# The last phase of a gated spectral/GEGLU backward kernel: the first way-back piece after two gate jobs, three kinds of loads on ScalarE's queue, ten b tiles ahead

## The chip, the cores and the metric

The kernel runs on one core of one Trainium2 chip. The metric is the device time of one execution in microseconds. Before the change the median of three runs is 1390.53 us (1386.52 to 1390.64).

The engines named below are TensorE (PE; its weight loads are PEld), VectorE (DVE), ScalarE (ACT), GpSimd (POOL) and SyncE (SP). Each executes its own instructions in order. DMA transfers are issued by SyncE, ScalarE or GpSimd, as one more instruction in that engine's stream; SPq, ACTq and POOLq mark these in the profile.

## The reference

```python
def _A_ref(x, w_r, w_i):                      # spectral mixer
    X = rfft2(x.astype(float32)); X = X * (w_r + 1j * w_i)
    return irfft2(X, s=(S, D)).astype(bfloat16)
def _B_ref(x, w_gate, w_up, w_down):          # GEGLU
    return (gelu(x @ w_gate) * (x @ w_up)) @ w_down
x = A_x
g = sigmoid((x * gate_w).sum(-1, keepdims=True))
out = g * _A_ref(x, A_w_r, A_w_i) + (1 - g) * _B_ref(x, B_w_gate, B_w_up, B_w_down)
# returned: out, and its vector-Jacobian product with grad_out for
# x, w_r, w_i, w_gate, w_up, w_down, gate_w
```

x and grad_out are 2048 x 576, w_gate and w_up 576 x 4608, w_down 4608 x 576, the spectral weights 2048 x 289, all in bfloat16.

## The kernel before, in words

The 2048 rows are 16 row tiles t of 128 rows. The kernel has two phases.

The first phase (up to 919.7 us in the profile) goes through the 4608 hidden columns in 18 groups of 256. It computes the hidden activations and their gradients, stores them to DRAM scratch (`scr`, three kinds: A for the down product, dHg and dHu for the two gradients), accumulates the three weight gradients, and in between performs the forward transforms of x and grad_out, the products with the spectral weights, and the first half of the transforms back. Their half-way result lies in DRAM as V (`scr_p1` for the output, `scr_p2` for the gradient of x).

The second phase, in which the whole change lies, makes the output and the gradient of x. Its work is a list of jobs, one at a time on TensorE (L1123 to L1126):

- a b job (`b_job`, L1301) multiplies row tile t of A with the down weights `wd_all`, in three `pin` tiles of 12 chunks, two blocks each (one for each half of the 576 columns). A block is 12 matmuls (L1194). ScalarE copies the result into `bo`;
- a g job and a u job (`x_half`) accumulate the gradient of x for row tile t, first from dHg with `wgT_all`, then from dHu with `wuT`, into one PSUM pair that is held from the g job to the end of the u job. `x_end` then has VectorE add the spectral part and the gate part to it (`x_pre` L1366, `x_out` L1371) and store it.

The order before is g0, g1, b0 to b7, u0, u1, b8, and then g_t, u_t, b_(t+7) for t from 2, without b when they are used up. The last row tile's g and u are one job ("x").

The pin tiles are loaded by transposing DMA on SyncE's queue (L1120), six buffers, always six ahead of the block that TensorE has finished (`ensure`). The order of these loads is the order of the jobs. On the same queue, ahead of the jobs, stand three loads of `wd_all` (L1139) and the first loads of V; one transposing load of a quarter of a third of `wuT` (L1153, 9 in all) stands ahead of each of the jobs 1 to 9.

Between the blocks lie the pieces of the way back, four for each row tile i (`piece`, L1259): k = 0 and 1 are `z_piece` for the output and the gradient (six matmuls of the folded V, called F, with the table `RT`, L1244, and a copy Z by ScalarE, L1246); k = 2 and 3 are `d_piece` (six matmuls of Z with the table `It`, L1254, and two ScalarE activations into `yo`, kept in `spec[0]` or `spec[1]`, L1256). A piece also issues what comes later: k = 0 and 1 load V for row i + 2 (`load_p`, L1210, on SyncE's queue), k = 1 and 2 have VectorE fold V of row i + 1 into F (`fold`, L1221 to L1237), and k = 3 calls `posts`. The tables RT and It are built at the start of the phase from GpSimd iotas, VectorE arithmetic in float tiles (`f32t`) and ScalarE sines (L222, L203).

`tick` (L1283) decides when a piece comes. It is called after each block; its counter advances by one, except in g0 and g1, where no b job has begun and it stays. A piece is taken when the counter has reached a threshold, which starts at 0 and is then moved 3 or 4 ahead. So the first piece comes after the first block of g0, and a row takes 14 blocks.

`post(t)` (L1314) is done once b job t and the row's output piece are there. It loads x and grad_out of the row tile (L1319, L1321, SyncE's queue), and has VectorE make the output row, the gate's derivative (`dlog`, from grad_out, L1331) and the gradient of gate_w (from x, L1335). `x_end(t)` needs `dlog` of its row.

PSUM gives the phase eight tiles, four pairs, shared by b jobs, gate and up jobs and pieces (`acc_pair`).

Of the kernel before, what the change touches and what calls it, by code (L numbers as in the profile page):

```python
# [11 lines left out]
BF16 = mybir.dt.bfloat16  # L12
# [7 lines left out]
S, D, DF = 2048, 576, 289  # L20
P, T = 128, 16
# [22 lines left out]
def eo(c):  # L44

    return slice(c, 512, 4)
# [278 lines left out]
def kernel(  # L325
# [4 lines left out]
    nc = tc.nc  # L330
    LD = nc.sync
# [3 lines left out]
    kw = dict(reuse_waits="tile")  # L335
# [9 lines left out]
    x_v = A_x[0].rearrange("(p t) d -> p t d", t=T)  # L345
    do_v = grad_out[0].rearrange("(p t) d -> p t d", t=T)
# [523 lines left out]
    for c in range(6):  # L870
        w = gwr[0:1, eo(c)] if c < 4 else gwr[0:1, 512:D]
# [58 lines left out]
    def want(pr):  # L930

        n0 = FIRST[-1]
        if pr < len(FIRST):
            return FIRST[pr]

        def load(n):

            return n + 0.5 * min(max(n - mid_at, 0), n_mid)
        share = load(n0) + (load(n_slots) - load(n0)) * (pr + 1 - len(FIRST)) / (LASTP - len(FIRST))
        n = n0  # L940
        while n < n_slots and load(n + 1) <= share + 1e-9:
            n += 1
        return int(min(n, n_slots) + 1e-9)
# [21 lines left out]
    for g in range(NG):  # L965
# [3 lines left out]
        for m in range(NPR):  # L969
            pr = g * NPR + m  # L970
            n = want(pr) - done[0]
# [64 lines left out]
            else:  # L1036
# [29 lines left out]
                jobs = carry + hs  # L1066
# [53 lines left out]
        LD.dma_start_transpose(tl[:], scr[k][t // 4][t % 4][:, f0 * P:(f0 + FCB) * P])  # L1120
        return tl

    jobs = [("g", t) for t in range(2)] + [("b", t) for t in range(8)] + [("u", t) for t in range(2)] + [("b", 8)]  # L1123
    for t in range(2, T):
        jobs += [("g", t), ("u", t)] + ([("b", t + 7)] if t + 7 < T else [])
    jobs[-2:] = [("x", T - 1)]  # L1126
    seq = [(k, t, f0) for kind, t in jobs for k in ((1, 2) if kind == "x" else ("bgu".index(kind),)) for f0 in range(0, NFC, FCB)]
    loaded = {}
# [25 lines left out]

    o0v = out_0[0].rearrange("(p t) d -> p t d", t=T)
    o1v = out_1[0].rearrange("(p t) d -> p t d", t=T)
    with tc.tile_pool(name="p2f", bufs=4, **kw) as p2f, \
         tc.tile_pool(name="p2bo", bufs=8, **kw) as p2bo, \
         tc.tile_pool(name="p2b", bufs=6, **kw) as p2b, \
         tc.tile_pool(name="sp", bufs=1, **kw) as sp, \  # L1160
         tc.tile_pool(name="p2s", bufs=4, **kw) as p2s, \
         tc.tile_pool(name="p2res", bufs=1, **kw) as p2res, \
# [11 lines left out]
        def f32t(dt=F32):  # L1174
            return p2f.tile([P, D], dt, tag="f32t", name="f32t")

        def b16t():
            return p2b.tile([P, D], BF16, tag="b16t", name="b16t")
# [9 lines left out]
        def acc_pair():  # L1188
            return [pacc.tile([P, 512], F32, tag="acc", name="acc") for _ in range(2)]
# [14 lines left out]
        srcs_v = [q[:].rearrange("g (k t c) l -> (g k) t c l", k=4, c=2) for q in (scr_p1, scr_p2)]  # L1204
        vp, ft, zt = {}, {}, {}
        spec = [{}, {}]

        def load_p(i, w):
            vp[i, w] = sp.tile([P, 2, DF], BF16, tag="Vp", name="Vp", bufs=4)
            LD.dma_start(vp[i, w][:], srcs_v[w][:, i])  # L1210

        def fold(i, w):
            v = vp.pop((i, w))
# [33 lines left out]

        def d_piece(i, w):
            Z = zt.pop((i, w))
            yo = spec[w][i] = sp.tile([P, D], BF16, tag=("ya", "yd")[w], name="yo", bufs=(3, 6)[w])  # L1250
            yv = yo[:].rearrange("p (q r) -> p r q", r=6)
            for b, ps in enumerate(acc_pair()):
                for r in range(3):
                    nc.tensor.matmul(ps[:, r * 96:(r + 1) * 96], lhsT=Z[0:2 * LQ, 3 * b + r, :], rhs=It[0:2 * LQ, 3 * b + r, :],  # L1254
                                     start=True, stop=True)
                nc.scalar.activation(yv[:, 3 * b:3 * b + 3], ps[:, 0:288].rearrange("p (r q) -> p r q", r=3), ACT.Copy,  # L1256
                                     scale=(SD2, 1.0)[w])

        def piece(i, k):  # L1259

            def f():
                (z_piece, d_piece)[k // 2](i, k % 2)
                if k == 0 and i + 2 < T:
                    load_p(i + 2, 0)
                if k == 1:
                    if i + 2 < T:
                        load_p(i + 2, 1)
                    if i + 1 < T:
                        fold(i + 1, 0)
                if k == 2 and i + 1 < T:  # L1270
                    fold(i + 1, 1)
                if k == 3:
                    posts()
            return f
        pieces = [piece(i, k) for i in range(T) for k in range(4)]
        for i in range(2):
            for w in range(2):
                load_p(i, w)
        for w in range(2):
            fold(0, w)  # L1280
        ticks = [0, 0]

        def tick(on):  # L1283
            ticks[0] += on
            if pieces and ticks[0] >= ticks[1]:
                pieces.pop(0)()
                ticks[1] = ticks[0] + 3 + len(pieces) % 2

# [2 lines left out]
                pieces.pop(0)()  # L1291

        bos = {}
        posted = [0]

        def posts():
            while posted[0] in bos and posted[0] in spec[0]:
                post(posted[0])
                posted[0] += 1

        def b_job(t):  # L1301
            bps = acc_pair()
            bo = bos[t] = p2bo.tile([P, D], BF16, tag="bo", name="bo")
            for f0 in range(0, NFC, FCB):
                At = loaded.pop((0, t, f0))
                for h in range(2):
                    block(bps[h], h, At, lambda r: wd_all[:, f0 + r], f0 == 0, f0 + FCB == NFC)
                    tick(1)
                    if f0 + FCB == NFC:
                        nc.scalar.copy(bo[:, h * 288:(h + 1) * 288], bps[h][:, :288])  # L1310
                used[0] += 1
                ensure()

        def post(t):  # L1314

            bo = bos.pop(t)
            a_t = spec[0][t]
            x_t = b16t()
            LD.dma_start(x_t[:], x_v[:, t, :])  # L1319
            do_t = b16t()  # L1320
            LD.dma_start(do_t[:], do_v[:, t, :])  # L1321
            tmpo = f32t()
            V.tensor_scalar(tmpo[:], bo[:], omg32[:, t:t + 1], None, op0=ALU.mult)
            o0 = b16t()
            V.scalar_tensor_tensor(o0[:], a_t[:], g32[:, t:t + 1], tmpo[:], op0=ALU.mult, op1=ALU.add)
            ST.dma_start(o0v[:, t, :], o0[:])
            diff = f32t()
            V.tensor_tensor(diff[:], a_t[:], bo[:], op=ALU.subtract)
            junk = f32t()
            dg = p2s.tile([P, 1], F32, tag="dg", name="dg")  # L1330
            V.scalar_tensor_tensor(junk[:], diff[:], 1.0, do_t[:], op0=ALU.mult, op1=ALU.mult, accum_out=dg[:])  # L1331
            gg = p2s.tile([P, 1], F32, tag="gg", name="gg")
            V.tensor_tensor(gg[:], g32[:, t:t + 1], omg32[:, t:t + 1], op=ALU.mult)
            V.tensor_tensor(dlog[:, t:t + 1], dg[:], gg[:], op=ALU.mult)
            V.scalar_tensor_tensor(gacc[:], x_t[:], dlog[:, t:t + 1], gacc[:], op0=ALU.mult, op1=ALU.add)  # L1335
            if t == T - 1:
                V.tensor_copy(gsplit[:, 0], gacc[:])
                V.tensor_tensor(gsplit[:, 1], gacc[:], gsplit[:, 0], op=ALU.subtract)
# [12 lines left out]
        def x_half(t, k):  # L1351
            if k == 1:
                accs[t] = acc_pair()
            for f0 in range(0, NFC, FCB):
                src = loaded.pop((k, t, f0))
                for h in range(2):
                    block(accs[t][h], h, src, wT(k, f0), k == 1 and f0 == 0, k == 2 and f0 + FCB == NFC)
                    tick(len(bos) + posted[0] > 0)
                used[0] += 1
                ensure()  # L1360
# [81 lines left out]
```

## Time and profile before

| | us |
|---|---|
| median of three runs | 1390.53 |
| lowest, highest | 1386.52, 1390.64 |
| profiled execution | 1392.35 |
| its span, first to last instruction | 1390.6 |
| TensorE busy (weight loads) | 1366.5 (906.6) |
| VectorE, ScalarE, GpSimd busy | 842.9, 751.4, 260.5 |
| second phase, start to end | 919.7 to 1390.6 |
| mean granted TensorE clock | 0.993 |

The busy times are sums over the span; TensorE's overlapping weight loads are counted by themselves. The granted clock is the share of the full TensorE clock that the throttle allowed. A view of waits has one row for each pair of a waiting line and the one that released it: total time, number, longest. A timeline row has the start, the length, the engine, the line, the operation, what it writes and reads, how often, and in brackets the idle time of its engine just before it with what ended it.

### The profile page before, as it was taken

The numbers are of one execution on the slowest core, as the hardware profiler recorded it, in microseconds if no ns is written. First come the engines' busy times: TensorE is split into PE (matmuls) and PEld (weight loads), VectorE is DVE, ScalarE is ACT, GpSimd is POOL, SyncE is SP. The second block draws the span as 40 slices with busy tenths as digits, with TensorE's granted clock in tenths as the row PEclk, the third lists the DMA queues.
The fourth block names the chain that finished last, engine by engine and source line by source line (L and its number), as shares of the span: only waits on it lengthen the run. The fifth ranks groups of instructions, "written<-read, shape, count | busy, mean of one in ns | idle before, by whom it ended". The sixth has DMA issues, their size and how long they took to land. (4 is left out here: it accounts for less than half of the span.)

```text
span 1390.6 us, 26580 instructions
## 1 busy us (share of the span) xinstructions
PE 1366.5 (98%) x10280; PEld 906.6 (65%) x10280; DVE 842.9 (61%) x1976; ACT 751.4 (54%) x1360; POOL 260.5 (19%) x508
## 2 busy tenths in 40 slices
PE   9999999999999999999999999969998999999998
PEld 7566656656655655665565565537876888888876
DVE  7886767767669786677678555542435464454300
ACT  7886677777667777676777666521232323223100
POOL 5211110110323452343252211100000000000000
PEclk9999999999999999999999999989999999999999
DMA  7435534535644654664574575589999878887773
GB/s 232 129 88 142 143 100 130 142 101 132 174 127 126 178 149 126 156 177 112 146 196 116 159 190 138 130 237 176 201 196 179 159 172 172 161 170 150 163 142 75
DMA packets 497396, 211.84 MB, mean 152 GB/s; under 512 B 307219, under 2 KB 488150, under 8 KB 497270
## 3 DMA queue, kind: packets, MB, share of 16 engines
q1 hardware_dynamic: 480148, 184.76, 58.0%
q0 software_dynamic: 14912, 24.24, 6.1%
q8 instruction: 80, 1.31, 0.4%
q10 hardware_dynamic: 2210, 1.15, 0.3%
q14 instruction: 46, 0.38, 0.1%
HBM read 43.13 MB, written 93.56 MB: 98 GB/s over the span
## 5 line engine op out<-in xcount | busy, mean ns | idle before, releaser
L1194 PEld LDWEIGHTS <-pin 128*128 128x128 bf16 x3456 | 336.5, 98 | 90.4 <-issue 5.4
L506 PE MATMUL xy<-wgu,xT 128*128 128x512 bf16 x1152 | 270.7, 380 | 0.0
L636 PE MATMUL wps<-dH,xn 128*128 128x512 bf16 x1152 | 265.6, 379 | 0.1
L636 PEld LDWEIGHTS <-xn 128*128 128x128 bf16 x1152 | 112.5, 98 | 126.6 <-issue 0.6
L506 PEld LDWEIGHTS <-xT 128*128 128x128 bf16 x1152 | 106.7, 98 | 133.2 <-issue 24.8
L1194 PE MATMUL acc<-wd_all,pin 128*128 128x288 bf16 x1152 | 149.2, 289 | 4.4 <-DVE b16t L1371 4.4
L643 POOL DMA_DIRECT2D out_dram<-dw x134 | 73.2, 550 | 416.4 <-ACT dw L587 398.9
L618 PE MATMUL wps<-dB,A 128*128 128x288 bf16 x1152 | 149.6, 286 | 0.0
L1194 PE MATMUL acc<-wgT,pin 128*128 128x288 bf16 x1152 | 147.9, 287 | 0.0
L1194 PE MATMUL acc<-wuT,pin 128*128 128x288 bf16 x1152 | 146.6, 286 | 0.4 <-DMA pin<-scr 0.3
L490 PE MATMUL z<-wdT,dOT 128*128 128x256 bf16 x1152 | 137.7, 273 | 0.0
L618 PEld LDWEIGHTS <-A 128*128 128x128 bf16 x1152 | 112.7, 98 | 34.2
L518 ACT ACTIVATE da<-z,omg 128x256 bf16<-128x256 f32 x288 | 112.3, 473 | 34.5 <-PE z L495 34.3
L1256 ACT ACTIVATE yo<-acc 128x288 bf16<-128x288 f32 x64 | 67.3, 1243 | 115.3 <-PE acc L1254 114.1
L490 PEld LDWEIGHTS <-dOT 128*128 128x128 bf16 x1152 | 112.5, 98 | 21.4 <-issue 0.2
L527 ACT CAST xb<-xy 128x512 bf16<-128x512 f32 x144 | 85.3, 592 | 48.2 <-PE xy L506 48.2
L1246 ACT CAST Z<-acc 98x384 bf16<-98x384 f32 x64 | 27.5, 482 | 129.6 <-PE acc L1244 129.6
L525 ACT ACTIVATE q<-xy 128x512 bf16<-128x512 f32 x144 | 88.3, 615 | 4.9 <-PE xy L506 3.4
L564 DVE TENSOR_TENSOR xb<-xb,sg 128x1024 bf16<-128x1024 bf16 x48 | 33.1, 690 | 94.4 <-ACT sg L556 94.4
L528 ACT CAST hu<-xy 128x512 bf16<-128x512 f32 x144 | 87.5, 607 | 0.0
L1331 DVE SCALAR_TENSOR_TENSOR f32t<-f32t,b16t 128x576 f32<-128x576 f32 x16 | 12.1, 759 | 119.5 <-DMA b16t<-in_grad_out_dram 119.5
L587 ACT CAST dw<-wps 128x512 bf16<-128x512 f32 x72 | 42.4, 590 | 66.9 <-PE wps L636 65.9
(523 smaller groups left out, 1743.7 us busy)
## 6 DMA issues: line engine op xcount, KB each, us to landing
scr<-dH SPq DMA_DIRECT2D x144, 256.0 KB, 3.7
scr<-A SPq DMA_DIRECT2D x72, 256.0 KB, 2.7
out_dram<-dw POOLq DMA_DIRECT2D x134, 64.0 KB, 2.2
wd_all<-in_B_w_down_dram SPq DMA_DIRECT2D x3, 1728.0 KB, 10.5
out_dram<-dwd POOLq DMA_DIRECT2D x34, 144.0 KB, 2.9
scr_p<-Vt SPq DMA_DIRECT2D x32, 144.5 KB, 2.5
Vp<-scr_p SPq DMA_DIRECT2D x32, 144.5 KB, 3.1
wgu<-in_B_w_gate_dram SPq DMA_DIRECT2D x18, 256.0 KB, 4.3
```

The costliest lines, as they stand in the source:

```text
L490: nc.tensor.matmul(zo(t), lhsT=dOT[:, ci, t, :], rhs=wdT[:, ci, :], start=(t % 4 < 2 and ci == 0), stop=False)
L506: nc.tensor.matmul(xy[k][:, t % 2, :], lhsT=xT[:, ci, t, :], rhs=wgu[:, ci, :], start=False, stop=(ci == 3))
L518: nc.scalar.activation(da[:, t, :], z[:, t % 2, t // 2, :], ACT.Copy, scale=omg32[:, 4 * m + t:4 * m + t + 1])
L525: nc.scalar.activation(q[:, h, :], xy[:, :, 0:FG], ACT.Square)
L527: nc.scalar.copy(xb[:, h, :], xy[:, :, 0:FG])
L528: nc.scalar.copy(hu[:, h, :], xy[:, :, FG:2 * FG])
L587: wcopy[0](out, in_)
L618: nc.tensor.matmul(wps[:, :288], lhsT=tl(0, t)[:, fch * P:(fch + 1) * P], rhs=dB[:, t, h * 288:(h + 1) * 288], start=(t == 0), stop=(t == ...
L636: nc.tensor.matmul(wps[:].rearrange("p a b -> p (a b)"), lhsT=xn[:, t, c * P:(c + 1) * P], rhs=kt[t // 4][1][:, t % 4].rearrange("p k f -> ...
L643: wst[0].dma_start(ov[:, c, fsl], dw[:, k, :])
L1194: nc.tensor.matmul(acc[:, :288], lhsT=src[:, r, :], rhs=w_of(r)[:, h * 288:(h + 1) * 288], start=(first and r == 0), stop=(last and r == F ...
L1256: nc.scalar.activation(yv[:, 3 * b:3 * b + 3], ps[:, 0:288].rearrange("p (r q) -> p r q", r=3), ACT.Copy, scale=(SD2, 1.0)[w])
```

## The change

The first way-back piece waits for the counter to reach 2, which it first does after the second block of b0. The loads of V, x and grad_out are issued by ScalarE instead of SyncE. Those of x and grad_out leave `post` and go into the piece k = 1 of the same row, into tiles of their own (two each). Ten b jobs stand ahead of u0 instead of eight; the rest of the b jobs follow at t + 9. Pools change to make room: three float tiles instead of four, nine `bo` instead of eight, four other bfloat16 tiles instead of six, two and five `yo` tiles instead of three and six. A piece is now taken only when the kept gradient rows in `spec[1]` leave room.

```diff
-    jobs = [("g", t) for t in range(2)] + [("b", t) for t in range(8)] + [("u", t) for t in range(2)] + [("b", 8)]
+    jobs = [("g", t) for t in range(2)] + [("b", t) for t in range(10)] + [("u", t) for t in range(2)] + [("b", 10)]
     for t in range(2, T):
-        jobs += [("g", t), ("u", t)] + ([("b", t + 7)] if t + 7 < T else [])
+        jobs += [("g", t), ("u", t)] + ([("b", t + 9)] if t + 9 < T else [])
...
-    with tc.tile_pool(name="p2f", bufs=4, **kw) as p2f, \
-         tc.tile_pool(name="p2bo", bufs=8, **kw) as p2bo, \
-         tc.tile_pool(name="p2b", bufs=6, **kw) as p2b, \
+    with tc.tile_pool(name="p2f", bufs=3, **kw) as p2f, \
+         tc.tile_pool(name="p2bo", bufs=9, **kw) as p2bo, \
+         tc.tile_pool(name="p2b", bufs=4, **kw) as p2b, \
...
         def load_p(i, w):
             vp[i, w] = sp.tile([P, 2, DF], BF16, tag="Vp", name="Vp", bufs=4)
-            LD.dma_start(vp[i, w][:], srcs_v[w][:, i])
+            nc.scalar.dma_start(vp[i, w][:], srcs_v[w][:, i])
...
-            yo = spec[w][i] = sp.tile([P, D], BF16, tag=("ya", "yd")[w], name="yo", bufs=(3, 6)[w])
+            yo = spec[w][i] = sp.tile([P, D], BF16, tag=("ya", "yd")[w], name="yo", bufs=(2, 5)[w])
...
                 if k == 1:
+                    load_xd(i)
                     if i + 2 < T:
                         load_p(i + 2, 1)
...
-        ticks = [0, 0]
+        ticks = [0, 2]
 
         def tick(on):
             ticks[0] += on
-            if pieces and ticks[0] >= ticks[1]:
+            if pieces and ticks[0] >= ticks[1] and len(spec[1]) < 5 - (len(pieces) % 4 == 1):
                 pieces.pop(0)()
                 ticks[1] = ticks[0] + 3 + len(pieces) % 2
...
+        xd = {}
...
+        def load_xd(t):
+            xd[t] = [p2b.tile([P, D], BF16, tag=n, name=n, bufs=2) for n in ("x_t", "do_t")]
+            for tl, v in zip(xd[t], (x_v, do_v)):
+                nc.scalar.dma_start(tl[:], v[:, t, :])
...
-            x_t = b16t()
-            LD.dma_start(x_t[:], x_v[:, t, :])
-            do_t = b16t()
-            LD.dma_start(do_t[:], do_v[:, t, :])
+            x_t, do_t = xd.pop(t)
```

## Prediction

> **What bounds the kernel now.** I began with the page: busy times, slices, granted clock.
>
> ```profile
> PE 1366.5 (98%) x10280; PEld 906.6 (65%) x10280; DVE 842.9 (61%) x1976; ACT 751.4 (54%) x1360; POOL 260.5 (19%) x508
> ...
> PEclk9999999999999999999999999989999999999999
> ```
>
> TensorE is the limit: 1390.6 - 1366.5 = 24.1 us of the span is all its idle time. One slice, the 27th (904 to 939 us), has less than the full clock. No change that leaves the matmuls alone can gain more than the idle time and what a low clock costs beside it. The waits of TensorE say where the idle time is:
>
> ```profile
> PE acc L1244 <- DVE F L1235: 12.9, 1, 12.9
> PE acc L1194 <- DVE b16t L1371: 4.4, 1, 4.4
> ...
> PE acc L1194 <- DMA pin<-scr: 0.3, 1, 0.3
> ```
>
> Two single waits, 12.9 and 4.4 us, hold nearly all of it, and both lie in the last phase (from 919.7 us). The timeline around the first:
>
> ```profile
> 919.90 1.63 PE L1194 MATMUL acc<-wgT,pin 128*128 128x288 bf16 x12
> ...
> 931.35 0.68 ACT L203 ACTIVATE It<-f32t 98x576 bf16<-98x576 f32 x1 [2.57 <-DVE f32t L184]
> ...
> 934.44 0.34 PE L1244 MATMUL acc<-RTt,F 128*98 128x128 bf16 x1 [12.90 <-DVE F L1235]
> ```
>
> After one block (12 matmuls) of the first gate job the first way-back piece stands in TensorE's stream, and its F is folded (from 932.35) only once the tables RT and It are built. Around the second:
>
> ```profile
> 1044.92 0.38 SPq L1321 DMA_DIRECT2D b16t<-in_grad_out_dram  x1
> ...
> 1049.14 0.76 DVE L1331 SCALAR_TENSOR_TENSOR f32t<-f32t,b16t 128x576 f32<-128x576 f32 x1 [15.07 <-DMA b16t<-in_grad_out_dram]
> ...
> 1052.36 7.26 PE L1194 MATMUL acc<-wd_all,pin 128*128 128x288 bf16 x36 [4.45 <-DVE b16t L1371]
> ```
>
> Job b8 needs the PSUM pair that u0 filled. VectorE empties it late (at 1051.84), since its stream stood 15.07 us in a post at a grad_out load that SyncE issued late. The clock, by stretches (after the length and the five busy times: granted clock, DMA share, GB/s):
>
> ```profile
> 1053.00:1056.00 3.00, 3.00 (x14) 1.92 (x13) 3.00 (x17) 0.00 (x0) 0.67 (x2) 0.50 1.12 203
> ```
>
> The stretch from 930 to 935 shows 0.50 too, and 935 to 940 shows 0.66. Each long wait is followed by matmuls at half clock, which count as busy and do not appear in the 24.1 us.
>
> **What goes.** Undisturbed, 48 of these matmuls take 5.88 us in the chain (0.1225 each) and the six of a piece 0.34. First wait: g0 needs 72 x 0.1225 + 0.34 = 9.16 us; from its start at 919.90 to the next matmul (L1185, 944.53) it took 24.63. Excess 15.47, of which 12.90 + 0.44 are waits and 2.1 the clock. Second: from the piece at 1047.41 to the piece at 1059.46 are 12.05 us for 0.34 + 36 x 0.1225 = 4.75. Excess 7.30: wait 4.45, clock 2.85. Third, 0.29 us at 1028.6 for a late pin tile. Sum 23.06 us.
>
> Clock: the Trainium skill (TensorE: Matmul & The Clock Gate, Part 1) says that about 3.4 us of idleness halve the clock and about 3.4 us of work restore it. By that the clock would have cost some 1.7 us twice, and the sum would be 21.5. The rows show 2.1 and 2.85; I keep the rows.
>
> **First piece.** The counter of blocks does not advance in g0 and g1 (no b job has begun), so with its threshold at 2 the first piece follows the second block of b0. Without stalls that is 919.90 + 2 x 8.82 + 0.41 (spreading gate_w) + 24 x 0.1225 = 940.9 us. F now depends on a longer chain. With three instead of four float buffers, the third angle block, which ended at 924.8, waits for the first sine (926.3), and the fourth follows it: I estimate the sine of It 1.1 us later, its end at 933.1 instead of 932.0. Only then does ScalarE, in order, issue the four first V loads, which SyncE had begun at 918.36. They take 2.1 us to land (the first five) to 5.4 (the slowest V load), and the fold takes 3.1 (first instruction 932.35, last end 935.45). So F is ready at 938.3 to 941.6: a wait of 0 to 0.7, say 1 us; I take 0. What else is due earlier: b0 at 937.9 instead of 953.7 needs wd_all, whose loads land by 917.9 + 12.9 = 930.8 at the latest; the second fold is ready by 945, its piece stands at 947.
>
> **SyncE's queue.** Its stream stands nearly without a gap from 938.75 to 1034:
>
> ```profile
> 1020.24 3.65 SPq L1153 DMA_TRANSPOSE wuT<-in_B_w_up_dram  x1
> 1024.00 3.42 SPq L1120 DMA_TRANSPOSE pin<-scr  x2
> 1027.53 0.52 SPq L1210 DMA_DIRECT2D Vp<-scr_p  x1
> 1028.14 1.65 SPq L1120 DMA_TRANSPOSE pin<-scr  x1
> ```
>
> The 7th pin tile was issued at 938.75 and the 31st at 1024.00: 85.25 us for eight jobs, 10.66 a job, against 9.37 a job on TensorE (953.71 to 1028.62, eight b jobs). So the lead fell 1.29 us a job until u0 waited. Out of this stretch go 5 V loads and 3 pairs of x and grad_out, 7.5 us with the gaps, 0.9 a job: 9.7, or a drift of 0.4. The start is less kind: the pins of b0 now queue behind wd_all, on which the third V load stood until 928.43. Pin 7 issued at 928.4 and landing in 5.3 (the median of that stretch) is there at 933.7, 4 us early; a tile of b1 is issued some 11 us ahead. With the drift at 0.4 it still has 8 us at b8, above the 5.3 of a landing: no wait. If not the issuing but the transfers bound, the drift stays 1.29 and TensorE waits about 2 us near b7, where the wuT loads end; two more b jobs ahead of u0 then let SyncE recover. I take 0 and keep 3.
>
> The Trainium skill (DMA: Bandwidth & Descriptors, "Issuing engines are not separate DMA queues") speaks against this part: transfers from all queues share the same 16 engines, and another issuing engine saves only issue time. The DMA share of 0.97 to 1.30 between 946 and 1046 makes that serious; by it the 2 us would be lost.
>
> **ScalarE's queue** receives 32 V loads at 0.53 and 16 pairs at 0.57 + 0.38: 32 us of issuing, beside 105.8 us of busy time in the 454 us from 936 to 1390. They stand behind the Z copies of their pieces, and the next copy is wanted 3 or 4 blocks later (4.4 us and more); a burst of three is 1.5 us. Their waits are old: a V buffer is free once the fold one row back has run, an x buffer once the post two rows back has run, 21 blocks (31 us) earlier. Cost 0; without this cover 32 us.
>
> **Posts, buffers, b order.** VectorE loses its waits for grad_out (119.5 us in all, 16 times), so u0 is emptied within a few us, while u1 occupies TensorE for 9.4: the 4.45 goes. x and grad_out are needed two pieces after their issue, 7 blocks or 10 us, against 5.0 us for the slowest landing of that tile. Ten b tiles move two jobs without adding one. The new cap on d outputs holds pieces from about the ninth row on; the last row falls on block 236 of 264 instead of 221, and no up job catches up with it, as rows stay three or more ahead. The smaller pools carry VectorE-ordered tiles. I take 0 for all of this, at most 1 us.
>
> **Sum.** 1392.35 (the profiled execution; span 1390.6) - 23.06 = 1369.3. That execution stands 1.8 above the median of the runs; from the median, 1390.53 - 23.06 = 1367.5. With half a microsecond for a late F or pin: **1368**. The fastest run gives 1386.52 - 23.06 = 1363.5.
>
> **Rivals.** (a) Small waits come in their place: F up to 1 us, pins up to 3, buffers 1: up to 1373. For it: the DMA share above and a margin near zero at the first piece. (b) One stall keeps its size: V loads from ScalarE land so late that the first piece waits 4.5 us again, or u0's pair is still emptied late because post stands at another load. Either costs 4.5 + 2.85: 1375. Against it: F has to be 4 us later than the slowest landing makes it. (c) The change doesn't do what it says: the first stall only moves to b0, which takes that VectorE's table work waits for TensorE; its rows wait for GpSimd and ScalarE only. Then 1390.53 - 7.30 - 0.29 = 1383, and with the second stall kept as well no change, 1390. (d) Slower: ScalarE's queue. If a load's issue there is held as SyncE's V load was (3.46 us at 918.36), bursts delay the Z, yo and bo copies, and TensorE waits for PSUM pairs, two of four being held by g0 and g1 and later by an up job. It decides from a burst over some 4.4 us, three blocks; above that every row pays. To lose 4.2 us on balance takes 27.3 us over 16 rows, 1.7 each: 6.1 us for three issues, against 1.5 by the rows. Time then 1395 and more.
>
> **Chances.** Forecast (1363 to 1371) 0.62; (a) above 1371, 0.14; (b) 0.10; (c) 0.06, half of it no change; (d) 0.08. A measurement of this kernel separates about 0.3%, 4.2 us, from no change: faster 0.89, within 0.03, slower 0.08. The range from 1362 to 1379 takes in the forecast, (a) and (b), with 1.5 us below the fastest run's figure.
>
> **What would show it.** Right: no wait on F or on L1371 over 1 us, granted clock 1.00 throughout from 920 us, g0 and g1 at 8.8 us each, no VectorE wait for grad_out, TensorE's idle time 3 us or less over the whole span. Wrong: a wait of TensorE for ScalarE's copies (d), for pin between b4 and b9 (a), for F at about 941 (b). The prediction fails as a whole if the last phase ends up bound by the DMA engines.

## The result, and the profile after

The changed kernel takes 1377.59 us (median of four runs, 1375.8 to 1381.87), the kernel before 1389.49 (1386.52 to 1390.64): ratio 0.9922, 95% interval 0.9893 to 0.9951. Repeated beside the experiments it took 1376.67 us, ratio 0.9918 (0.9900 to 0.9936). The gain is 11 to 12 us, about half of the 22.5 that were forecast; the time lies inside the range. The profiled executions, 1392.35 before and 1375.8 after, are 16.55 apart; the first is slower than all four timed runs before, the second the fastest of its four, so the pair shows more than the medians.

The page after, busy times and granted clock:

```profile
PE 1354.6 (99%) x10199; PEld 905.7 (66%) x10280; DVE 844.1 (61%) x1976; ACT 751.6 (55%) x1360; POOL 259.8 (19%) x508
...
PEclk9999999999999999999999999999999999999999
```

No slice is visibly slow any more. The matmul count is 81 lower than before, the weight loads are the same 10280: records are missing from this profile, and the 7.5 us "issue" rows of the waits below (47 times at most 0.2 us, all at L506, where 66 records are missing) are such holes, not waits: the weight loads of the missing matmuls are all there. TensorE's waits after:

```profile
PE xy L506 <- issue: 7.5, 47, 0.2
PE acc L1244 <- DVE gwf L1186: 4.6, 1, 4.6
PE pf L868 <- POOL ident masks.py:199: 1.4, 1, 1.4
```

The waits for F (12.9) and for L1371 (4.4) are gone, and so is the one for pin. A new one stands at the first piece: 4.6 us, and the engine named is VectorE at gwf, the gate weights spread over the partitions. The timeline there:

```profile
937.38 3.10 PE L1194 MATMUL acc<-wd_all,pin 128*128 128x288 bf16 x24
...
938.41 0.36 DVE L1221 TENSOR_TENSOR pm<-Vp 128x196 f32<-128x196 bf16 x1 [5.08 <-DMA Vp<-scr_p]
...
944.55 0.82 DVE L1186 COPY gwf<-acc 128x288 f32<-128x288 f32 x2
...
945.06 0.88 PE L1244 MATMUL acc<-RTt,F 128*98 128x128 bf16 x6 [4.58 <-DVE gwf L1186]
945.73 8.45 PE L1194 MATMUL acc<-wd_all,pin 128*128 128x288 bf16 x48
```

VectorE waits for the first V until 938.41, folds twice (to 944.5) and only then copies gwf out of PSUM. The next piece came at 954.02, 8.96 us after the first, where 0.34 + 48 x 0.1225 = 6.22 would do. So the place costs 4.58 + 2.74 = 7.32 us, the second part by the clock (0.50 between 945 and 950). From the first gate matmul to the end of the last one the phase took 451.1 us after and 467.1 before: 16.0 less, and 16.0 + 7.3 = 23.3 against the 23.06 worked out. In the profiled pair, then, one new wait with its slow clock accounts for what is short of the forecast.

### The profile page after: what moved, and what is told of

It reads as the page before. It is cut to its first block, busy times and chain, and to the rows that moved or that the text cites. A ratio compares the mean times of both kernels' runs of the same rounds, so it can differ in the third digit from the quotient of the medians.

```text
span 1374.0 us, 26478 instructions
## 1 busy us (share of the span) xinstructions
PE 1354.6 (99%) x10199; PEld 905.7 (66%) x10280; DVE 844.1 (61%) x1976; ACT 751.6 (55%) x1360; POOL 259.8 (19%) x508
## 4 chain that ended last, share of the span: by engine, by line
PE 94%; DVE 2%; DMA 1%; issue 1%; ACT 1%; SPq 0%; ACTq 0%; POOL 0%; DVEq 0%; POOLq 0%
PE acc L1194 30%; PE xy L506 17%; PE wps L636 17%; PE wps L618 10%; PE z L490 9%; PE wps L650 2%; PE xy L499 2%; PE z L495 2%; DMA wd_all<-in_B_w_down_dram 1%; PE acc L1244 1%; PE pf L679 1%; PE acc L1254 1%; PE pf L697 1%; PE pf L682 1%; PE pf L839 1%
## 5 line engine op out<-in xcount | busy, mean ns | idle before, releaser
L506 PE MATMUL xy<-wgu,xT 128*128 128x512 bf16 x1086 | 258.7, 379 | 8.5 <-issue 7.5
L506 PEld LDWEIGHTS <-xT 128*128 128x128 bf16 x1152 | 106.8, 98 | 133.1 <-issue 24.8
L1375 DVE TENSOR_TENSOR b16t<-acc,f32t 128x288 bf16<-128x288 f32 x32 | 14.7, 458 | 175.9 <-PE acc L1194 175.9
## 6 DMA issues: line engine op xcount, KB each, us to landing
scr_p<-Vt SPq DMA_DIRECT2D x32, 144.5 KB, 2.6
Vp<-scr_p ACTq DMA_DIRECT2D x32, 144.5 KB, 4.3
```

The source lines that it names most:

```text
L506: nc.tensor.matmul(xy[k][:, t % 2, :], lhsT=xT[:, ci, t, :], rhs=wgu[:, ci, :], start=False, stop=(ci == 3))
```

## The experiments

All times are medians; each ratio is to runs of the kernel before on the same chip beside it (their medians: 1387.93 to 1390.26 us). Runs on different chips are compared by these ratios; where the medians say something else, both are given.

**The order on VectorE.** The changed kernel, with the two first folds behind the copies of gwf:

```diff
-        for w in range(2):
-            fold(0, w)
...
             if i == 1:
                 spread_gw()
+                for w in range(2):
+                    fold(0, w)
```

> The changed kernel with one move: the first two folds stand in VectorE's stream behind the two copies of the spread gate weights (gwf) instead of ahead of them. Theory 1 (the first piece waits for the PSUM pair of the spread gate weights, which VectorE empties only behind both folds): the copies run at about 933 us, the pair is free, and the piece waits only for its F, ready at about 941.5 against 940.5: the wait falls from 4.6 to about 1 us and the clock stays full, so the time falls by 6 to 7 us against the changed kernel, to about 1371. Theory 2 (F itself is late because ScalarE issues the first V loads late, and the copies are only the last of several that were late together): the wait stays at 4 us or more, and the time at 1377 to 1378.

1372.67 us (1371.51 to 1374.69), ratio 0.9891 (0.9876 to 0.9906). The first piece's wait is gone: gwf is copied at 933.93, F is ready at 939.8, the piece runs at 940.89 after two blocks of b0:

```profile
933.93 0.82 DVE L1186 COPY gwf<-acc 128x288 f32<-128x288 f32 x2
...
939.48 0.35 DVE L1237 SCALAR_TENSOR_TENSOR F<-wp__11796 128x196 bf16<-128x196 f32 x1
...
940.89 0.50 PE L1244 MATMUL acc<-RTt,F 128*98 128x128 bf16 x6
```

Theory 1 holds for the order. V also landed sooner here (936.74 instead of 938.41), so this run alone doesn't say how late F would have been; the repeat of the changed kernel, below, does. By the medians the time fell by 4 to 5 us against the changed kernel (the intervals of the ratios overlap a little), not 6 to 7, for another wait took a place. TensorE's waits have this row:

```profile
PE acc L1254 <- ACT bo L1315: 3.9, 2, 2.6
```

and ScalarE's timeline shows where the first of the two comes from (ACTq rows are loads that it issues):

```profile
947.64 0.34 ACTq L1299 DMA_DIRECT2D x_t<-in_A_x_dram  x1
947.84 0.48 ACT L1246 CAST Z<-acc 98x384 bf16<-98x384 f32 x1
948.93 0.34 ACTq L1299 DMA_DIRECT2D do_t<-in_grad_out_dram  x1
952.59 0.33 ACTq L1210 DMA_DIRECT2D Vp<-scr_p  x1
952.96 0.40 ACT L1315 CAST bo<-acc 128x288 bf16<-128x288 f32 x1 [4.63 <-DMA wuT<-in_B_w_up_dram]
```

Three loads, from the first issue to the end of the last, take 5.3 us, where the same three took 1.42 in the changed kernel's profile (954.56 to 955.98). The copy of bo stands behind them, and TensorE waits 1.27 us for its pair; the second such burst took 6.4 us (993.01 to 999.41), with 2.58 us of waiting. This is rival (d) of the prediction, in small: two bursts, not sixteen.

**The first V loads.** The changed kernel, with the four first V loads on SyncE's queue:

```diff
-        def load_p(i, w):
+        def load_p(i, w, q=nc.scalar):
-            nc.scalar.dma_start(vp[i, w][:], srcs_v[w][:, i])
+            q.dma_start(vp[i, w][:], srcs_v[w][:, i])
...
-                load_p(i, w)
+                load_p(i, w, LD)
```

> The changed kernel with the four first V loads back on SyncE's queue, ahead of the seventh pin tile; all later V, x and grad_out loads stay on ScalarE's. Both theories on the first piece have V landed by 933, the folds from 933.3 to 939.4, the gate weights copied by 940.2, and the piece at 940.5 without a wait: 7 us faster than the changed kernel, about 1370. Where SyncE's queue is the limit, the pin tiles of b0 to b2 come 4 to 7 us later and waits for pin appear before u0, up to 3 us; where it isn't, none appear.

1374.78 us (1370.52 to 1377.12), ratio 0.9904 (0.9888 to 0.9920). No wait at the first piece, as both theories had it; waits of 1.0 and 0.8 us for ScalarE, none for pin. Of the 7 us expected the medians show 2 to 3, and the interval overlaps that of the changed kernel. The profiled execution, 1370.52, is the fastest of its runs: what the slower ones wait for it cannot show.

**Both moves together.**

> Both moves: the gate weights copied ahead of the folds, and the first V loads on SyncE's queue. Theory 1 and theory 2 alike: no wait of TensorE over 0.5 us in the last phase, granted clock 1.00, 7.3 us faster than the changed kernel, about 1370. If the first stall has a third cause (tables, wd_all), 3 us or more of wait remain.

1375.31 us (1374.31 to 1376.91), ratio 0.9910 (0.9897 to 0.9923). The first piece is clear, but the sum is no better than either move, and the expectation (no wait over 0.5 us, about 1370) failed. Its waits:

```profile
PE acc L1194 <- DMA pin<-scr: 3.8, 2, 2.5
```

and 1.2 us for ScalarE. With the first stall removed by either way, some 2 to 5 us of small waits appear before u0 in the three profiles, at other places each time.

**The threshold alone.** The kernel before with one edit:

```diff
-        ticks = [0, 0]
+        ticks = [0, 2]
```

> The kernel before with the later first piece alone (threshold 2); queues, pools, b order stay. The first stall goes: V is loaded by SyncE, the folds end by 938.4, the gate weights are copied by 939.2, and the piece stands at 940.9: no wait, 15.5 us gained. The second stall (wait 4.45, clock 2.85) stays. If SyncE's issuing is the limit (10.66 us a job against 9.37), the pins have 8 us of lead at b1 and run dry from about b3: 1.3 us of waiting a job, about 6 in all before u0, and the gain is 9: about 1380. If the transfers hide it, no pin waits, gain 15.5: about 1374.

1373.04 us (1372.13 to 1376.97), ratio 0.9899 (0.9883 to 0.9914): no less than the whole change. Two of TensorE's waits, and VectorE's for grad_out:

```profile
PE acc L1194 <- DMA pin<-scr: 4.1, 4, 1.6
...
PE acc L1194 <- DMA wuT<-in_B_w_up_dram: 0.6, 1, 0.6
```

```profile
DVE f32t L1331 <- DMA b16t<-in_grad_out_dram: 119.0, 16, 18.2
```

The pins do run dry with all loads on SyncE's queue, by 4.1 us where some 6 were expected. The second stall, expected to stay, is gone, although VectorE waits for grad_out as long as before (119.0 us, once 18.2). Its stream around u0's evacuation (L1371):

```profile
1020.55 0.76 DVE L1331 SCALAR_TENSOR_TENSOR f32t<-f32t,b16t 128x576 f32<-128x576 f32 x1 [18.23 <-DMA b16t<-in_grad_out_dram]
...
1029.28 0.82 DVE L1371 TENSOR_TENSOR b16t<-acc,f32t 128x288 bf16<-128x288 f32 x2
1030.02 0.51 DVE L1323 TENSOR_SCALAR f32t<-bo,omg 128x576 f32<-128x576 bf16 x1
```

The long wait is that of row 2's post; row 3's post (from 1030.02) stands behind the evacuation.

**All but the threshold.** The changed kernel with `ticks = [0, 0]`:

> The changed kernel with the threshold back at 0: all of the change except the later first piece. The first stall returns, longer than before, since F now waits for V loads that ScalarE issues late: the piece stands at 920.8 and F comes at 941 to 942, a wait of 20 us in place of 12.9, and 2 to 3 us of slow clock; the gate weights' copies don't matter, as no pair is short yet. The second stall stays away. Against the changed kernel (4.6 us and clock) some 14 to 16 us more: about 1391, no faster than the kernel before. Rival: if the first V loads were late by chance only, the wait is 13 us and the time about 1384.

1389.27 us (1386.22 to 1392.84), ratio 0.9995 (0.9982 to 1.0009): no gain.

```profile
PE acc L1244 <- DVE F L1235: 15.2, 1, 15.2
```

The second stall is away, the first is 2.3 us longer than before (15.2, not the 20 expected: V landed sooner here), and small waits of 2.3 us are added. Of the 7.3 us that the loads, the b order and the pools win at the second place, these waits take back 4.6. The run doesn't show that the early loads are what removed the second stall: with ten b tiles the order on VectorE is another too, row 4's post (1061.66) stands behind u0's evacuation (1059.82 and 1061.29). V landed 2.2 us after its issue here, with TensorE standing and a DMA share of 0.50 (932 to 935), and 6.1 us after it in the changed kernel (0.94), where a wuT load runs meanwhile (931.87 to 935.46) and pin tiles follow.

**Why the second stall went.** The kernel before with `ticks = [0, 1]`:

> The kernel before with the threshold at 1 instead of 0 or 2, and nothing else. The first piece stands behind one block of b0, at about 939.5, with F ready at 935.5: no first stall. Theory of the order: at threshold 1 the third row's post (rows counted from 0) still comes after the 54th block, the last of u0, and so ahead of u0's evacuation in VectorE's stream, as in the kernel before; the evacuation waits for grad_out again, and the ninth b job waits 3 to 6 us for VectorE with 2 to 3 us of slow clock. Time 5 to 8 us above the run with threshold 2: 1378 to 1381. Theory of lateness: the second stall went in the threshold-2 run because without the first stall the loads stand differently on SyncE's queue, and one block makes no difference: no wait for L1371, and 1373 as there.

1378.06 us (1377.48 to 1379.07), ratio 0.9927 (0.9912 to 0.9942): 5 us more than with threshold 2, for one block. The timeline at the ninth b job:

```profile
1036.39 0.76 DVE L1331 SCALAR_TENSOR_TENSOR f32t<-f32t,b16t 128x576 f32<-128x576 f32 x1 [13.98 <-DMA b16t<-in_grad_out_dram]
...
1039.10 0.82 DVE L1371 TENSOR_TENSOR b16t<-acc,f32t 128x288 bf16<-128x288 f32 x2
...
1039.61 0.33 PE L1244 MATMUL acc<-RTt,F 128*98 128x128 bf16 x3 [2.25 <-DVE b16t L1371]
```

The order decides. With threshold 0 or 1, the post of row 3 comes within u0's last blocks and stands ahead of u0's evacuation on VectorE, which inherits its wait for grad_out. With threshold 2 it comes one block after u0 and stands behind it, as shown above; what stands ahead, row 2's post with its wait of 18.2 us, is done before u0's matmuls are. The wait here is smaller than the 3 to 6 us expected, with 1.7 us of slow clock (36 matmuls in 6.24 us, against 4.57 for 36 at full clock).

**Eight b tiles.** The run with the folds behind gwf, in the b order of before (`b` to 7 ahead of u0, then t + 7):

> The folds behind the gate weights' copies (as in the run of that name), and the b order of the kernel before: eight b tiles ahead of the first up job. Theory: ten b tiles bring nothing by themselves, since the second stall went with the early grad_out loads and the pins have lead enough: 1371 to 1374, as with ten. Rival: the two extra b jobs are what keeps u0 and the ninth b job clear: the wait for VectorE before b8 (4.45 us and the clock) comes back, or waits for pin or wuT of 3 us or more at u0: 1376 to 1380.

1373.77 us (1371.36 to 1377.86), ratio 0.9902 (0.9882 to 0.9922), against 0.9891 with ten: the times don't tell them apart. The profiled execution, the slowest of them, shows the rival's wait, and a wait for F at the first piece:

```profile
PE acc L1194 <- DMA wuT<-in_B_w_up_dram: 3.1, 1, 3.1
PE acc L1244 <- DVE F L1235: 2.0, 1, 2.0
...
PE acc L1244 <- DVE F L1236: 0.5, 1, 0.5
```

u0 comes as the last wuT lands. At the first piece gwf had been copied (935.85), but V came late: ScalarE began the sine of It at 934.75, 2.5 us later than in the changed kernel's profile, and V landed 6.1 us after its issue. A clock of 0.51 followed (945 to 948). So with the order mended the first piece can still wait, for F. The wait for VectorE before the ninth b job does not return.

**The queue of the loads.** The same base, all V, x and grad_out loads on SyncE's queue (`LD` for `nc.scalar`) or on GpSimd's (`ST`):

> The folds behind the gate weights' copies, and every V, x and grad_out load on SyncE's queue, at the same early places in the program. If SyncE's issuing is the limit before u0, the pins run dry and TensorE waits 4 to 8 us for pin, no longer for ScalarE's copies: 1374 to 1378. If the shared DMA engines are the limit, whichever queue issues, the waits sum to about the same as with ScalarE's queue (3 to 4 us): 1372 to 1374.

> The folds behind the gate weights' copies, and every V, x and grad_out load on GpSimd's queue, which is nearly idle in this phase and on whose stream only stores stand. If the waits of TensorE for ScalarE's bo copies (3.9 us in the first of these runs) come from loads whose issue is held on ScalarE's queue, they vanish, and no wait takes their place: 1369 to 1370. If the DMA engines are simply full, waits for pin of 3 to 4 us come instead, and the time stays at 1372 to 1374. The first V loads no longer wait for the sine of It, so F is ready earlier too.

SyncE: 1375.03 us (1372.97 to 1375.55), ratio 0.9901 (0.9883 to 0.9919), waits for pin 3.3 us in four places, none for ScalarE. GpSimd: 1372.63 (1370.28 to 1378.13), ratio 0.9891 (0.9871 to 0.9911), waits for pin 1.7, none for ScalarE. ScalarE, above: 0.9891, waits for bo 3.9. The waits for bo belong to ScalarE's queue, but without them the time is the same: another wait comes. Neither expectation fits whole: on SyncE's queue the waits are the 3 to 4 us of full DMA engines and the time that of the issuing limit, on GpSimd's the time is as expected for full engines and the waits are less.

**Fewer transfers at a time.** The wuT loads spread over eleven jobs, with the loads on GpSimd's and on ScalarE's queue:

```diff
-            if i > 0 and wT_loads:
+            if i % 4 and wT_loads:
```

> The run with all loads on GpSimd's queue, and in addition the nine wuT loads spread over eleven jobs instead of nine (none at the 4th and the 8th), which the ten b tiles leave room for. If what is left of the waits comes from DMA engines that are full while the wuT loads run, the waits for pin (1.7 us there) go to below 0.5 and the runs come closer together: 1369 to 1371. If it comes from single late transfers, nothing changes: 1372 to 1373.

> The run with the folds behind the gate weights' copies (loads on ScalarE's queue) and the nine wuT loads spread over eleven jobs. If the holding of loads on ScalarE's queue comes from full DMA engines during the wuT loads, it falls by a part only, since jobs with a wuT load are as full as ever: TensorE still waits 1 to 4 us for bo copies, 1371 to 1373. If the holding comes from a backlog that builds up over the jobs, it goes: 1369 to 1370, the same as on GpSimd's queue.

GpSimd: 1372.49 us (1368.58 to 1373.58), ratio 0.9865 (0.9847 to 0.9882); its profile has 3.0 us of waits for pin, one of 2.4 at u0, where 1.7 stood without the spreading, and the median time is that of the run without it (1372.63); only the ratio is lower, the kernel before having taken 1390.26 us on this chip and 1387.93 on that one. So the first expectation failed, and on GpSimd's queue the spreading shows no gain in time. ScalarE: 1370.33 us (1369.69 to 1371.38), ratio 0.9853 (0.9836 to 0.9869), the best of all, clear of the changed kernel's interval and of the same kernel without the spreading (2.3 us less by the medians, some 5 by the ratios). Its waits of the last phase:

```profile
PE acc L1194 <- DMA pin<-scr: 0.6, 1, 0.6
PE acc L1244 <- DVE F L1236: 0.5, 1, 0.5
```

No wait for bo is left, and the time is that of the second expectation, a backlog which the two jobs without a wuT load let drain. That it was a backlog is not shown: a burst of 4.3 us is still there (1036.97 to 1041.28), where the first expectation had the holding fall by a part only.

**The changed kernel again.**

> The changed kernel unaltered, as the yardstick for this call. If the first piece's wait of 4.6 us is the order of VectorE's stream (both folds ahead of the gate weights' copies, which empty the PSUM pair), it is there again at 3 to 6 us, with the slow clock behind it, and the time is 1376 to 1378. If it came from one late landing by chance, it is gone and the time is 1371.

1376.67 us, as reported above. In its profiled execution (1373.14, its fastest) the first piece waits 1.6 us for gwf, not 3 to 6, and a pin costs 2.2: V landed at 935.93 instead of 938.41, 2.5 us sooner with the same issue.

```profile
938.68 0.35 DVE L1237 SCALAR_TENSOR_TENSOR F<-wp__11709 128x196 bf16<-128x196 f32 x1
...
942.07 0.82 DVE L1186 COPY gwf<-acc 128x288 f32<-128x288 f32 x2
```

```profile
939.82 1.14 PE L1194 MATMUL acc<-wd_all,pin 128*128 128x288 bf16 x8
942.58 0.63 PE L1244 MATMUL acc<-RTt,F 128*98 128x128 bf16 x5 [1.62 <-DVE gwf L1186]
```

Here F was ready at 939.0, before the two blocks of b0 ended (941.0), so the wait is the PSUM pair's alone. The order on VectorE is a fixed cause; the length of the wait goes with the landing of V.

## Why the prediction was right, and where its size failed

**First piece: the step that failed.** "I take 0" for the wait rested on F alone. F's bounds held (938.3 to 941.6; the fold ended at 941.5), and so did the 1.1 us of later table work: the sine of It began at 932.24, 0.9 later. That the bounds held is in part luck, of two errors against each other: the V loads were issued from 932.26, as the sine began and not at its end (933.1), and the first took 6.1 us to land, more than the 5.4 of the slowest one before. But a piece needs a PSUM pair too. With g0, g1 and b0 holding three of the four, the pair of the spread gate weights is the one left, and its two copies stood behind both folds on VectorE. That order was in the kernel before as well, where nobody needed the pair. The step should have asked of each operand of the moved matmul, its output first, when it is free. The cost, 4.58 + 2.74 us, is what rival (b) said (4.5 + 2.85) for a different reason. So the time falls inside the stated range by the price of a rival that had 0.10, and not by the forecast (up to 1371, 0.62); the first-piece step failed in what it waits for.

**What goes.** The 23.06 us were right: the last phase is 16.0 us shorter in the profile with the new stall of 7.3 in it. The reading ahead of them, that two waits hold nearly all of TensorE's 24.1 us of idle time, was too strong (they are 17.3), but nothing was worked out from it. Matmuls at half clock, which no wait shows, made up 5 of the 23.

**Posts, b order.** The second stall went, and VectorE's wait for grad_out is 0.4 us instead of 119.5, as predicted. But the early loads were not needed for TensorE's sake: the threshold moves the post behind u0's evacuation, and the threshold alone gives 0.9899. Whether the early loads would do it without a change of the order, no run shows: in each run that has them, the post stands behind the evacuation. The prediction had the wait right and missed that its place in VectorE's stream was part of the cause. Ten b tiles bring no time that the runs resolve by themselves; they give the spread wuT loads room.

**SyncE's queue.** "I take 0 and keep 3" was about right: no wait for pin in the changed kernel's profile, 2.2 in its repeat. The rate estimate carries over: with the loads on SyncE's queue the pins run dry (4.1 and 3.3 us). With them elsewhere the waits for pin go from none to 3.8 us, the most with the first V loads on SyncE's queue and both moves. The rule of the Trainium skill that was weighed there, that another issuing engine saves issue time only (DMA: Bandwidth & Descriptors, "Issuing engines are not separate DMA queues"), agrees with the runs as far as they go: ScalarE's, SyncE's and GpSimd's queue give 0.9891, 0.9901 and 0.9891, with overlapping intervals. Fewer transfers at a time gave 0.9853 on ScalarE's queue, and on GpSimd's no shorter time.

**ScalarE's queue.** "Cost 0" held in the changed kernel's profile and not in the run with the folds moved, where bursts of 5.3 and 6.4 us were followed by waits of 1.27 and 2.58 for bo. The 4.4 us from which rival (d) was to decide fits both; that it happens in sixteen rows does not.

**What stays open.** The median gained 10.6 us less than forecast (11.9 against 22.5), and the profiled wait explains 7.3. The rest may be the small waits that differ from profile to profile, and a later V at the first piece; the slower executions of the changed kernel were not profiled, so this is not shown.

## What to carry to other kernels

When a matmul is moved, list when each thing it needs is free: operands, and above all the PSUM tile it writes, whose release can stand behind unrelated work in another engine's stream. Where an in-order engine waits for a load, what is queued right behind decides what the wait costs; one block's shift in the program removed 5 us without any load coming sooner. When a long stall is removed, the transfers that it hid have to fit into less time: count them for that stretch, and try to spread those that have slack: here that helped on one queue of two, while moving the loads from queue to queue changed the place of the waits and not the time.

## What the runs showed of the hardware that was not expected

A load's issue can be held for microseconds on a queue that does little else: a V load of 144.5 KB on ScalarE's queue was issued 3.3 us after the load before it (949.27 to 952.59), the compute instruction behind it waiting all that time, while the transposes on SyncE's queue ran with a DMA share of 1.19 (930 to 1030 us). What held it is not shown: in the changed kernel's profile the share was 1.13 in the same stretch, and no burst of the three loads took more than 2.5 us.

The clock did not follow the length of a wait alone. After a wait of 2.25 us (threshold 1) it was 0.76 and then 0.63 until 1045 (the row below), and after one of 2.03 us with another of 0.53 behind it (eight b tiles, first piece) 0.51, while after waits of 2.58, 2.47 and 3.09 us (folds moved, both moves, eight b tiles at u0) it stayed at 1.00:

```profile
1042.00:1045.00 3.00, 3.00 (x17) 2.04 (x16) 3.00 (x18) 0.00 (x0) 0.55 (x2) 0.63 1.08 255
```

The Trainium skill (TensorE: Matmul & The Clock Gate, Part 1) speaks of a free-running window of about 3.4 us, with the clock halved after at least one idle window. All five waits are shorter than that, so read as windows idle from end to end the rule has the clock fall after none of them. It fell after the two shortest of the five (after a still shorter one, 1.62 us in the repeat of the changed kernel, it did not), and what tells them from the others stays open.
